# Half-height transposes in two banks and spread inverse sums in an attention and MLP kernel

## The chip, the core and the metric

The kernel runs on one core of one Trainium2 chip. Its engines have queues of their own: TensorE (PE, matmuls; PEld are its weight loads), VectorE (DVE), ScalarE (ACT), GpSimd (POOL) and SyncE (SP), which here issues the DMAs. The metric is the device time of one execution in microseconds, lower is better.

## What is computed

Rotary attention over 4 batches, 8 heads, 576 positions and 64 dimensions, then a layer norm and an MLP of 512 to 2,048 to 512 on the joined heads, with a residual:

```python
q_rot, k_rot = (rotate(q), rotate(k))
scores = scale * np.matmul(q_rot, k_rot.transpose(0, 1, 3, 2))
scores = scores - np.max(scores, axis=-1, keepdims=True)
attn = np.exp(scores)
attn = attn / (np.sum(attn, axis=-1, keepdims=True) + 1e-09)
attn_out = np.matmul(attn, v)
x = attn_out.transpose(0, 2, 1, 3).reshape(B, S, H * D)
mu = np.mean(x, axis=-1, keepdims=True)
var = np.mean((x - mu) ** 2, axis=-1, keepdims=True)
xn = (x - mu) / np.sqrt(var + 1e-06) * g_ln
out = x + np.maximum(xn @ w_ch1, 0.0) @ w_ch2
```

## The kernel before

**Attention** (`attention(i)`) runs over 16 pairs of heads, two heads j on partitions 0 to 63 and 64 to 127. A pair has four query tiles c of 128 queries and a last one (c = 4) of 64 queries, in which the two heads share a tile. For each tile TensorE makes the scores (L419, L415 for c = 4) into one `sc` buffer per head, VectorE takes the row maximum (L460), and ACT the exponential with the row sums (L472). The exponentials `p` have queries on partitions, and the product with v needs keys there, so TensorE transposes them: per tile and head four blocks of 128 x 128 into one `t` bank (`tr`, L516), copied out to `pt` by ACT or VectorE (L285 through `cp_`); the 64 keys left over per two tiles (`tail`, L536); and for c = 4 blocks of 64 rows (`last`, L555 and L556). The product with v (`pv`, L604 for the leftover keys, L608 for the others) goes over part a = 0 (256 queries) and a = 1 (320). It is scaled by the inverse sums into `xt` (L618).

**The inverse sums** stand one per partition and are needed along the free axis, the same on 64 partitions. Before: epsilon is added (L482 on ACT, L484 on VectorE), VectorE inverts (L488), TensorE transposes the 4 or 5 columns to rows (L574), they are copied to `row`, written to DRAM (L586), and read back spread over 64 partitions (L596, L598) into `inv`.

**Banks.** The accumulator memory has eight banks. Three score buffers have two each, `t` has two, used in turn by transposes, products with v and row transposes. When the sum for the layer norm of block 0 is made, the third score buffer is given up for two banks `m` (`share`), for layer norm and MLP.

**The MLP.** Tokens stand in five blocks. Block 0 is multiplied plainly in 32 units (`mlp_unit`, L872, 12 matmuls a unit) in between attention; the other four blocks go in pairs after it (L1025). In the background the weights are decoded and split by VectorE, ACT and GpSimd (L748 to L833).

**The order.** The program is a list of tasks with engines, costs in us, due times (`prio`), things waited for (`after`) and banks or buffers that they `take` and `give`. `Plan.run` goes through them in order of due time and starts the first that could start now, and writes its instructions; each engine then keeps that order. `ORDER` is a list of seeds by which due times are shifted.

## Time and profile before

| | us |
|---|---|
| median of 3 runs | 695.56 |
| the runs | 2233.5, 695.04, 695.56 |
| the profiled execution | 695.15 |
| its span, first to last instruction | 693.4 |

| engine | busy us of the span | instructions |
|---|---|---|
| PE | 672.1 (97%) | 3,954 |
| VectorE | 517.1 (75%) | 856 |
| GpSimd | 416.7 (60%) | 318 |
| ACT | 376.3 (54%) | 805 |

Busy is the union of the instructions' durations. TensorE's are pipelined, so a duration holds latency that overlaps the next instruction; the distance between two starts tells what one step costs. A float32 matmul of the program is two instructions in the trace (two passes), a transpose is one. The span has three parts: attention alone up to some 130 us, attention with block 0's MLP units up to 406, and the paired products after that.

### The profile page before, as it was taken

To read this page: it belongs to the slowest core of one execution; us is meant where nothing else is said; L and a number is where in the kernel's file an instruction comes from. 1 tells how busy PE (TensorE), PEld (TensorE's weight loads), DVE (VectorE), ACT (ScalarE), POOL (GpSimd) and SP (SyncE) were. 2 spreads that over 40 slices of the span, in tenths; PEclk is the share of its full clock that TensorE was granted. 3 is DMA by queue.
4 is the path that set the end of the run, shared out by engine and by line. 5 is a ranking of instruction groups with operands and counts; after the bars stand their busy time and mean duration, and the time that the engine had idled before them with its cause. 6 is when DMAs were issued, how large, how long until landed. Compare 5 with 4: busy or idle time off the path is not lost.

```text
span 693.4 us, 11541 instructions
## 1 busy us (share of the span) xinstructions
PE 672.1 (97%) x3954; PEld 507.2 (73%) x3954; DVE 517.1 (75%) x856; ACT 376.3 (54%) x805; POOL 416.7 (60%) x318
## 2 busy tenths in 40 slices
PE   6989999999999999999999999999999999999997
PEld 5555555666666666666666669989999999999996
DVE  4788878787877777778776758886867868757574
ACT  2677768766669675778675644341434234414130
POOL 4568775667779498787793614761457717415153
PEclk8899999999999999999999999999999999999999
DMA  8355664545847776577675347659668886666663
GB/s 267 123 186 175 200 218 164 176 158 185 293 159 249 252 239 243 174 248 251 242 238 196 108 152 244 214 184 307 215 215 264 268 268 208 221 215 212 213 213 133
DMA packets 85323, 147.20 MB, mean 212 GB/s; under 512 B 10880, under 2 KB 56592, under 8 KB 85264
## 3 DMA queue, kind: packets, MB, share of 16 engines
q1 hardware_dynamic: 85264, 146.45, 63.7%
q8 instruction: 32, 0.52, 0.3%
q14 instruction: 27, 0.22, 0.1%
HBM read 108.60 MB, written 37.82 MB: 211 GB/s over the span
## 4 chain that ended last, share of the span: by engine, by line
PE 88%; DVE 5%; ACT 4%; issue 1%; DMA 1%; SPq 1%; DVEq 0%; ACTq 0%
PE n L1025 40%; PE m L872 12%; PE sc L419 9%; PE t L608 8%; PE t L516 8%; PE sc L415 3%; PE t L604 2%; DVE mx L460 1%; ACT p L472 1%; PE t L555 1%; PE t L536 1%; ACT pt L285 1%; PE m L668 1%; DVE total L484 1%; DVE ws L833 1%
## 5 line engine op out<-in xcount | busy, mean ns | idle before, releaser
L1025 PE MATMUL n<-x,w 128*128 128x448 f32 x672 | 140.2, 367 | 0.0
L1025 PEld LDWEIGHTS n<-x,w 128*128 128x128 f32 x672 | 125.5, 188 | 12.2 <-issue 1.1
L460 DVE TENSOR_REDUCE mx<-sc 128x1 f32<-128x576 f32 x144 | 104.6, 750 | 32.1 <-PE sc L419 24.9
L472 ACT ACTIVATE p<-sc,mx 128x576 f32<-128x576 f32 x144 | 106.0, 740 | 32.1 <-DVE mx L460 27.5
L1025 PE MATMUL n<-o,w 128*128 128x448 f32 x576 | 121.3, 369 | 0.0
L1025 PEld LDWEIGHTS n<-o,w 128*128 128x128 f32 x576 | 107.8, 188 | 11.2 <-issue 0.5
L952 ACT ACTIVATE o<-tmp 128x448 fp32r<-128x448 f32 x96 | 55.3, 579 | 105.4 <-PE n L1025 38.8
L959 POOL TENSOR_TENSOR o<-tmp,o 128x448 fp32r<-128x448 f32 x53 | 66.3, 1269 | 43.8 <-ACT o L952 43.7
L419 PE MATMUL sc<-xk,xq 64*128 64x288 f32 x512 | 85.8, 438 | 4.3 <-DVE xk L338 3.0
L516 PE MATMUL t<-ident,p 128*128 128x128 f32 x512 | 78.3, 285 | 7.0 <-DVE pt L285 1.9
L516 PEld LDWEIGHTS t<-ident,p 128*128 128x128 f32 x512 | 57.0, 143 | 37.9 <-issue 12.6
L285 ACT COPY pt<-t 128x512 f32<-128x512 f32 (+1 forms) x99 | 54.4, 552 | 53.9 <-PE t L516 46.8
L757 POOL TENSOR_TENSOR fw<-fw,w 128x512 int32<-128x512 int32 x32 | 42.9, 1345 | 46.4 <-ACT w L751 20.9
L608 PE MATMUL t<-pt,v 128*64 128x320 f32 (+1 forms) x512 | 69.1, 412 | 0.0
L419 PEld LDWEIGHTS sc<-xk,xq 64*128 64x128 f32 x512 | 48.2, 190 | 25.8 <-issue 10.6
L1097 DVE TENSOR_TENSOR xt<-xt,n 128x448 f32<-128x448 f32 x80 | 48.5, 615 | 18.7 <-PE n L1025 18.4
L608 PEld LDWEIGHTS t<-pt,v 128*64 128x64 f32 x512 | 33.9, 136 | 31.3 <-issue 12.3
L872 PE MATMUL m<-xh,w 128*128 128x512 f32 x128 | 47.8, 417 | 0.0
L872 PE MATMUL m<-hh,w 128*128 128x512 f32 x128 | 47.7, 416 | 0.0
L1084 POOL TENSOR_TENSOR tmp<-tmp 128x448 f32<-128x448 f32 x15 | 20.3, 1354 | 44.9 <-DVE tmp L1063 39.8
L388 POOL TENSOR_TENSOR xs<-xs,rope_sb 128x576 f32<-128x576 f32 x30 | 45.0, 1505 | 1.4 <-DVE mx L460 1.4
L285 DVE COPY pt<-t 128x512 f32<-128x512 f32 (+1 forms) x61 | 37.0, 613 | 10.2 <-PE t L516 6.6
(119 smaller groups left out, 1149.7 us busy)
## 6 DMA issues: line engine op xcount, KB each, us to landing
w<-s SPq DMA_DIRECT2D x64, 512.0 KB
w<-v SPq DMA_DIRECT2D x96, 256.0 KB
s<-ws SPq DMA_DIRECT2D x32, 512.0 KB
xs<-in_qk SPq DMA_DIRECT2D x30, 288.0 KB
w<-in_w1p SPq DMA_DIRECT2D x16, 512.0 KB
v<-w SPq DMA_DIRECT2D x16, 512.0 KB
w<-in_w2p SPq DMA_DIRECT2D x16, 512.0 KB
v<-in_vp SPq DMA_DIRECT2D x16, 320.0 KB
```

Source lines behind the costliest of these rows:

```text
L285: (ACT.copy if plan.engine == "ACT" else DVE.tensor_copy)(o, i)
L388: eng().tensor_tensor(out=x[step], in0=x[step], in1=rope_sb[:, step], op=ALU.mult)
L419: PE.matmul(ps[:, a, :HS], lhsT=q[r, c * P : (c + 1) * P], rhs=k[r, KEYS[a]], start=True, stop=True)
L460: DVE.tensor_reduce(out=mx, in_=st["ps", i, n][:, :, :HS], axis=AX.XY, op=ALU.max, negate=True)
L472: ACT.activation(out=halves(p), in_=st.pop(("ps", i, n))[:, :, :HS], func=AF.Exp, bias=st.pop(("mx", i, n)), scale=1.0, accum_out=total)
L516: PE.transpose(ps[:, k], p[:, j, j * T + k * P : j * T + (k + 1) * P], ident)
L608: PE.matmul(ps[r], lhsT=v[:, k, r], rhs=pt[:, j, k], start=False, stop=k == 3)
L872: PE.matmul(ps, lhsT=wt, rhs=x, start=c + m == 0, stop=c + m == NC + 1)
L952: ACT.activation(out=o[0], in_=x(), func=AF.Relu if relu else AF.Copy)
L959: eng().tensor_tensor(out=lo, in0=x(), in1=raw(hi), op=ALU.subtract)
L1025: PE.matmul(ps, lhsT=wt, rhs=x, start=fresh and kc + z == 0, stop=kc + z == 3, skip_group_check=True)
L1097: DVE.tensor_tensor(out=o, in0=o, in1=ps(which, h), op=ALU.add)
```

## The change

- A tile's transposes of both heads become one task. Each 128 x 128 block is transposed as two halves of 64 rows (64 queries), the first on the array's upper 64 rows into bank 0 of a fixed tile `turned`, the second on the lower 64 rows into bank 1. The group takes both `t` banks; each half is copied out by an instruction of its own. The tails and the last tile are made in the same manner.
- The inverse sums are spread by products: the column of inverses, repeated 64 times, is the stationary operand and the identity the moving one (`spread`, L612 and L615 of the new program), and one copy brings the result to `inv`. Row transposes, row copies and the DRAM round trip go.
- The leftover keys of the product with v are multiplied per head, 64 output columns at a time, like the other keys.
- From pair 4 on, spread products and products with v take `m` banks instead of `t`. `m` is made when the scores of pair 3 are done.
- The planner has modes of the array, S (64 rows), V (64 columns) and M (whole), with costs of a change, and prefers to stay in one; costs are set anew, and `ORDER` is another list with other kinds of shifts.

```diff
--- before.py
+++ after.py
+ROWS = slice(0, D), slice(D, 2 * D)
...
 ORDER = [
...
-SHARE = 0.08, 0.01, 0.1, 0.3, 0.3
+SHARE = 0.08, 0.01, 0.1, 0.3, 0.3, 1.0, 1.0
 OVER = {"PE": 0.0, "DVE": 0.08, "ACT": 0.1, "POOL": 0.045, "NONE": 0.0}
+SWITCH = {("S", "M"): 0.2, ("M", "S"): 0.19, ("S", "V"): 0.3, ("V", "S"): 0.2, ("V", "M"): 0.2, ("M", "V"): 0.1}
+RUN = {"M": 5.0, "S": 0.0, "V": 0.0}
+STAY = {"M": 0.0, "S": 8.0, "V": 8.0}
...
+                if e == "PE":
+                    if kept is None and t.mode != mode:
+                        kept = t, e, picked
+                        most = float("inf") if now - since < RUN[mode] else t.prio + STAY[mode]
+                        continue
+                    if kept is not None and (t.mode != mode or t.prio > most):
+                        continue
...
+                if e == "PE":
+                    t.end += SWITCH.get((mode, t.mode), 0.0)
+                    since, mode = now if mode != t.mode else since, t.mode
...
-    scp, tp = passing("sc", space=PSUM), passing("t", RINGS["t"], space=PSUM)
+    scp, tp = passing("sc", space=PSUM), passing("t", space=PSUM)
+    turned = tp.tile([P, 2, 512], F32, name="t")
...
-    rows = {(i, a): dp.tile([4 + a, P], F32, name=f"sums{i}_{a}") for i in range(NP) for a in range(2)}
...
-            return add({"DVE": 0.19}, g, [add({"ACT": 0.22, "DVE": 0.12}, f, [exps[n] for n in units], N)], N)
+            return add({"DVE": 0.19}, g, [add({"ACT": 0.28, "DVE": 0.16}, f, [exps[n] for n in units], N, port=True)], N)
...
+        ring = "t" if i < NPB else "m"
...
-            qs = slice(c * P - PARTS[a].start, (c + 1) * P - PARTS[a].start)
-            trans = []
-            for j in range(2):
-                def tr(j=j, c=c):
-                    ps = st["tp", i, c, j] = bank_t(i, j).rearrange("p (k n) -> p k n", k=4)
-                    p = st["p", i, c]
+            def tr(c=c):
+                p = st["p", i, c]
+                for j in range(2):
                     for k in range(4):
-                        PE.transpose(ps[:, k], p[:, j, j * T + k * P : j * T + (k + 1) * P], ident)
-                def cp_(j=j, c=c, a=a, qs=qs):
-                    copy(alloc(a)[0][:, j, :, qs], st.pop(("tp", i, c, j)))
-                tt = add({"PE": 0.47}, tr, [exps[2 * c + j]], N + 0.1 * j, take=[ring_t(i, j)], lag=0.2, name=f"t{i}.{c}.{j}")
-                trans.append(tt)
-                take = [f"pt{a}"] if c % 2 == 0 and j == 0 else []
+                        for h, r in enumerate(ROWS):
+                            PE.transpose(turned[:, h, (4 * j + k) * D : (4 * j + k + 1) * D], p[r, j, j * T + k * P : j * T + (k + 1) * P], ident[r, r])
+            def cp_(h, c=c, a=a):
+                at = c * P - PARTS[a].start + h * D
+                copy(alloc(a)[0][:, :, :, at : at + D], turned[:, h].rearrange("p (j k n) -> p j k n", j=2, k=4))
+            tt = add({"PE": 0.47}, tr, [exps[2 * c], exps[2 * c + 1]], N, take=["t", "t"], lag=0.2, name=f"t{i}.{c}", mode="S")
+            trans = [tt]
+            for h in range(2):
+                take = [f"pt{a}"] if c % 2 == 0 and h == 0 else []
                 deps = [tt] + ([parts[a][0]] if parts[a] else [])
...
+                parts[a].append(add(how_c, lambda h=h, f=cp_: f(h), deps, N + 0.1 * h, take=take, give=["t"], of=tt, gid=h, name=f"c{i}.{c}.{h}"))
...
             def tail(c=c):
-                ps = st["tp", i, c, 2] = tp.tile([P, 512], F32, name="t")
                 for n in range(2):
-                    p = st.pop(("p", i, c - 1 + n))
-                    PE.transpose(ps[:, n * P : (n + 1) * P], p.rearrange("p j s -> p (j s)")[:, S - T : S + T], ident)
+                    p = st.pop(("p", i, c - 1 + n)).rearrange("p j s -> p (j s)")
+                    for h, r in enumerate(ROWS):
+                        PE.transpose(turned[:, h, n * D : (n + 1) * D], p[r, S - T : S + T], ident[r, r])
             def tail_copy(c=c, a=a):
-                ps = st.pop(("tp", i, c, 2))
-                copy(alloc(a)[1][:, : 2 * P], ps[:, : 2 * P])
+                o = alloc(a)[1][:, : 2 * P].rearrange("p (n h x) -> p h n x", n=2, h=2)
+                copy(o, turned[:, :, : 2 * D].rearrange("p h (n x) -> p h n x", n=2))
             dep = trans + first_trans + [exps[2 * c + 1], first_exp]
...
+            tt = add({"PE": 0.13}, tail, dep, N + 0.3, take=["t", "t"], give=["p", "p"], lag=0.2, name=f"tl{i}.{c}", mode="S")
+            t2 = add({"ACT": 0.40, "DVE": 0.42}, tail_copy, [tt, parts[a][0]], N + 0.3, give=["t", "t"], of=tt)
             parts[a].append(t2)
...
+        def last():
+            p = st.pop(("p", i, 4))
+            for k in range(4):
+                for j, r in enumerate(ROWS):
+                    PE.transpose(turned[:, j, k * T : (k + 1) * T], p[r, j * T + k * P : j * T + (k + 1) * P], ident[r, r])
+            for j, r in enumerate(ROWS):
+                PE.transpose(turned[0:T, j, 4 * T : 5 * T], p[r, (S - T, 0)[j] : (S, T)[j]], ident[r, r])
+        tt = add({"PE": 0.30}, last, [exps[8]], N, take=["t", "t"], give=["p9"], lag=0.2, name=f"tz{i}", mode="S")
+        for j, r in enumerate(ROWS):
             def last_copy(j=j, r=r):
-                ps = st.pop(("tp", i, 4, j))
                 pt, p4 = alloc(1)
-                copy(pt[:, j, :, 2 * P : 2 * P + T], ps[:, : 4 * T].rearrange("p (k q) -> p k q", k=4))
-                copy(p4[r, 2 * P : 2 * P + T], ps[0:T, 4 * T : 5 * T])
-            tt = add({"PE": 0.42}, last, [exps[8]], N + 0.1 * j, take=[ring_t(i, j)], give=["p9"] if j else [], lag=0.2, behind=[tt] if j else [], name=f"tz{i}.{j}")
+                copy(pt[:, j, :, 2 * P : 2 * P + T], turned[:, j, : 4 * T].rearrange("p (k q) -> p k q", k=4))
+                copy(p4[r, 2 * P : 2 * P + T], turned[0:T, j, 4 * T : 5 * T])
             d = 0.58
...
+            parts[1].append(add({"ACT": d, "DVE": d + 0.05}, last_copy, [tt, parts[1][0]], N + 0.1 * j, give=["t"], of=tt, gid=j))
...
...
+            def one_bank():
+                return turned[:, plan.task.got["t"][0]] if ring == "t" else bank()
+            def spread(a=a):
+                t = st.pop(("sums", i, a))
+                iv = st["spread", i, a] = one_bank()[:, : PARTS[a].stop - PARTS[a].start]
+                for c in range(2):
+                    for j, r in enumerate(ROWS):
+                        PE.matmul(iv[r, c * P : (c + 1) * P], lhsT=t[:, 2 * c + j : 2 * c + j + 1].broadcast_to([P, D]), rhs=ident, start=True, stop=True)
+                if a:
+                    for j, r in enumerate(ROWS):
+                        PE.matmul(iv[r, 2 * P :], lhsT=t[:, 4:5].broadcast_to([P, D]), rhs=ident[:, r], start=True, stop=True)
+            def spread_copy(a=a):
                 if a == 0:
                     st["inv", i] = smp.tile([P, S], F32, name="inv", bufs=RINGS["inv"])
...
+                copy(st["inv", i][:, PARTS[a]], st.pop(("spread", i, a)))
             def pv(a=a):
                 (pt, p4), v = st.pop(("pt", i, a)), st["v", i]
-                s = PARTS[a]
-                ps = st["pv", i, a] = tp.tile([P, s.stop - s.start], F32, name="t")
-                PE.matmul(ps, lhsT=v[:, 4], rhs=p4, start=True, stop=False)
-                for k in range(4):
-                    for j in range(2):
-                        r = slice(j * D, (j + 1) * D)
-                        PE.matmul(ps[r], lhsT=v[:, k, r], rhs=pt[:, j, k], start=False, stop=k == 3)
+                ps = st["pv", i, a] = one_bank()[:, : PARTS[a].stop - PARTS[a].start]
+                for k in range(5):
+                    for j, r in enumerate(ROWS):
+                        PE.matmul(ps[r], lhsT=v[:, k, r], rhs=pt[:, j, k] if k < 4 else p4, start=k == 0, stop=k == 4)
             def scale(a=a):
                 s = PARTS[a]
...
                     DVE.tensor_tensor(out=o, in0=ps[:, x], in1=st["inv", i][:, lo - b * S : hi - b * S], op=ALU.mult)
             N = nominal(i, 3 if a == 0 else 8) + 5
...
+            there = [ev["shared"]] if ring == "m" else []
+            rt = add({"PE": 0.46 if a == 0 else 0.58}, spread, [inverse[a]] + there, nominal(i, 3 if a == 0 else 8) + 0.6, take=[ring], lag=0.2, name=f"sp{i}.{a}", mode="V")
+            rd = add({"ACT": 0.36 + 0.05 * a, "DVE": 0.42 + 0.06 * a}, spread_copy, [rt] + ([rd] if a else []), nominal(i, 3 if a == 0 else 8) + 0.6, take=["inv"] if a == 0 else [], give=[ring], of=rt)
+            t = add({"PE": 2.16 if a == 0 else 2.73}, pv, parts[a] + [ev["v", i]] + there, N, take=[ring], give=[f"pt{a}"] + (["v"] if a else []), lag=0.2, name=f"pv{i}.{a}", mode="V")
             fresh = [n for n, lo, hi in pieces(b, a) if cc == 0 and lo == BLOCKS[n][0]]
             lead = [ev["fresh", n] for n, lo, hi in pieces(b, a) if n not in fresh]
...
+            ev["x", i, a] = add({"DVE": 0.5}, scale, [t, rd], N, behind=lead, take=["xt"] * len(fresh), give=[ring] + (["inv"] if a else []), of=t)
...
-            ev["shared"] = add({"NONE": 0.0}, share, [t3], -1e3, take=["sc"], which=RINGS["sc"] - 1)
-        mt = t = add({"PE": 0.92 * f}, mean, [t3, ev["c3"], ev["shared"]], N, take=["m"], lag=0.2, name=f"ln{n}")
+            pass
+        mt = t = add({"PE": 0.86 * f}, mean, [t3, ev["c3"], ev["shared"]], N, take=["m"], lag=0.2, name=f"ln{n}")
...
     for i in range(1, NP):
+        if i == NPB:
+            ev["shared"] = add({"NONE": 0.0}, share, [ev["s", (i - 1, 4)]], -1e3, take=["sc"], which=RINGS["sc"] - 1)
```

The new order at three places. First TensorE (PE) in the middle of attention, with MLP units around. Before, scores (L419) stand between two groups of whole transposes (L516), then the leftover product (L604) and the others with v (L608):

```order
L516 MATMUL t<-ident,p 128x128 x4
L419 MATMUL sc_115<-xk,xq 128x288
L419 MATMUL sc_114<-xk,xq 128x288
L419 MATMUL sc_115<-xk,xq 128x288
L419 MATMUL sc_114<-xk,xq 128x288
L516 MATMUL t<-ident,p 128x128 x4
L604 MATMUL t<-p_2103,v 128x320
L608 MATMUL t<-pt_2102,v 64x320 x8
L516 MATMUL t<-ident,p 128x128 x4
```

In the changed program the same work, scores (L460), half transposes (L550), product with v (L627), reads:

```order
L460 MATMUL sc_115<-xk,xq 128x288
L460 MATMUL sc_116<-xk,xq 128x288
L460 MATMUL sc_115<-xk,xq 128x288
L460 MATMUL sc_116<-xk,xq 128x288
L550 MATMUL t<-ident,p 128x64 x16
L627 MATMUL m<-pt_1625,v 64x320 x8
L627 MATMUL m<-p_1626,v 64x320 x2
```

Two groups of four whole transposes have become one of 16 halves behind the scores, the product with v goes to `m`, and its leftover keys come last.

Second, TensorE where the inverse sums are turned, before (L574 is the row transpose, L872 an MLP group, L536 a tail of transposes):

```order
L574 MATMUL t<-ident,total_2197 4x128
L872 MATMUL m<-xh,w 128x512
L872 MATMUL m<-xl,w 128x512
L872 MATMUL m<-xh,w 128x512 x2
L872 MATMUL m<-xl,w 128x512
L872 MATMUL m<-xh,w 128x512
L536 MATMUL t<-ident,p 128x128 x2
```

and in the changed program (L550 are half transposes, L612 is the spread product, L891 an MLP group):

```order
L550 MATMUL t<-ident,p 128x64 x16
L612 MATMUL m<-ident,total_1751 64x128 x4
L891 MATMUL m<-xh,w 128x512
L891 MATMUL m<-xl,w 128x512
L891 MATMUL m<-xh,w 128x512 x2
L891 MATMUL m<-xl,w 128x512
```

The row transpose of four columns into a `t` bank has become four products with the identity into an `m` bank, behind a group of half transposes and ahead of the MLP groups.

Third, SP's queue in the early pairs, before (L586 writes rows of sums, L596 and L598 read them back, L739 and L781 move weights, L380 loads q and k):

```order
L739 DMA w_449<-in_w1p 128x1024
L781 DMA v_181<-w 128x1024
L586 DMA sums_1_118<-row_464 5x128
L739 DMA w_511<-in_w1p 128x1024
L596 DMA inv<-sums_1_118 64x2x128
L598 DMA inv<-sums_1_118 64x64
L596 DMA inv<-sums_1_118 64x2x128
L598 DMA inv<-sums_1_118 64x64
L586 DMA sums_0_119<-row_553 4x128
L781 DMA v_182<-w 128x1024
L596 DMA inv<-sums_0_119 64x2x128 x2
```

and in the changed program (L758 and L800 move weights, L421 loads q and k, L439 v):

```order
L800 DMA v_150<-w 128x1024
L758 DMA w_491<-in_w1p 128x1024
L439 DMA v<-in_vp 128x640
L758 DMA w_598<-in_w1p 128x1024
L421 DMA xk<-in_qk 128x576
L421 DMA xs<-in_qk 128x576
L421 DMA xq<-in_qk 128x576
L421 DMA xs<-in_qk 128x576
```

The loads stand one behind the other, with no transfer of sums between them.

## Rows read from the trace of the kernel before

**Rows 1.** Busy time by stretch: us, then each engine's busy us, TensorE's clock, DMA.

```profile
20.00:100.00 80.00, 73.28 (x501) 44.56 (x497) 67.77 (x117) 59.29 (x141) 57.55 (x41) 0.98 0.58 190
100.00:405.00 305.00, 301.20 (x1963) 196.71 (x1961) 234.25 (x399) 214.96 (x480) 218.98 (x162) 1.00 0.61 209
405.00:665.00 260.00, 260.00 (x1321) 233.77 (x1318) 188.81 (x292) 93.04 (x168) 119.12 (x95) 1.00 0.71 227
```

**Rows 2.** The page's chain that ended last, share of the span by engine.

```profile
PE 88%; DVE 5%; ACT 4%; issue 1%; DMA 1%; SPq 1%; DVEq 0%; ACTq 0%
```

**Rows 3.** The chain from 20 to 100 us, shares by line, largest first.

```profile
by line: PE sc L419 20.3%; PE t L516 16.0%; PE t L608 13.3%; DVE mx L460 7.9%; PE sc L415 5.6%; issue 5.0%; DVE total L484 4.4%; PE t L604 3.9%; DVE pt L285 3.9%; DVE fw L760 3.1%; PE t L536 2.2%; PE t L555 2.0%; DVE fw L823 2.0%; ACT pt L2
```

**Rows 4.** TensorE's longest waits, 20 to 100, then 100 to 405: us, times, longest.

```profile
PE t L516 <- ACT pt L285: 1.4, 2, 1.2
...
PE t L516 <- DVE pt L285: 1.1, 1, 1.1
```

**Rows 5.** TensorE in order of time: start, us, line, out<-in, shapes, count.

```profile
122.44 1.16 PE L697 MATMUL m<-std,quarter 128*128 128x128 f32 x8 [0.42 <-DVE std L692]
...
123.44 0.60 PE L516 MATMUL t<-ident,p 128*128 128x128 f32 x4
123.88 0.38 PE L536 MATMUL t<-ident,p 128*128 128x128 f32 x2
124.19 1.24 PE L419 MATMUL sc<-xk,xq 64*128 64x288 f32 x8
125.36 1.09 PE L516 MATMUL t<-ident,p 128*128 128x128 f32 x8
...
127.81 1.95 PE L608 MATMUL t<-pt,v 128*64 128x256 f32 x16
129.68 1.19 PE L415 MATMUL sc<-xk,xq 64*64 64x288 f32 x8
```

**Rows 6.** TensorE in windows cutting into a score group and a product with v.

```profile
133.57 0.65 PE L419 MATMUL sc<-xk,xq 64*128 64x288 f32 x4
...
133.81 0.41 PE L419 MATMUL sc<-xk,xq 64*128 64x288 f32 x2
...
128.29 0.60 PE L608 MATMUL t<-pt,v 128*64 128x256 f32 x4
...
128.50 0.60 PE L608 MATMUL t<-pt,v 128*64 128x256 f32 x4
```

**Rows 7.** Half transposes, on one row half, then on both, in order of time.

```profile
113.66 0.46 PE L555 MATMUL t<-ident,p 64*128 64x64 f32 x4
113.96 0.22 PE L556 MATMUL t<-ident,p 64*64 64x64 f32 x1
...
136.50 0.28 PE L555 MATMUL t<-ident,p 64*128 64x64 f32 x3
136.56 0.22 PE L556 MATMUL t<-ident,p 64*64 64x64 f32 x1
136.62 0.22 PE L555 MATMUL t<-ident,p 64*128 64x64 f32 x1
136.68 0.22 PE L556 MATMUL t<-ident,p 64*64 64x64 f32 x1
```

**Rows 8.** Groups by line and shape, 100 to 405: busy us, mean ns, idle before.

```profile
L285 DVE COPY pt<-t 128x512 f32<-128x512 f32 x31 | 20.9, 682 | 4.5 <-PE t L516 4.5
...
L484 DVE TENSOR_SCALAR total<-total 128x4 f32<-128x4 f32 x8 | 7.1, 884 | 2.3 <-ACT p L472 2.1
...
L285 DVE COPY p<-t 128x256 f32<-128x256 f32 x14 | 5.9, 420 | 3.9 <-PE t L536 3.8
...
L285 ACT COPY pt<-t 128x512 f32<-128x512 f32 x61 | 35.6, 586 | 37.0 <-PE t L516 36.7
```

**Rows 9.** The chain in order of time, whole program: start, us, what.

```profile
403.99 2.30 PE t L608 x16
...
466.36 223.12 PE n L1025 x1086
```

More of the change, by code (lines that the diff above doesn't have):

```diff
@@ L97, in reorder @@
+        if what in ("wait", "lean"):
+            size *= 0.1
+        together = 2 * chance(seed, 9) - 1
+        for i in range(lo, hi):
             t = tasks[i]
-            if later and "SP" not in t.how:
+            if what == "release" and "SP" not in t.how:
                 continue
-            k = kind[i] + 1000003 if mode in (0, 4) else i
-            if chance(seed, 2 * k + 100) < SHARE[mode]:
+            if what == "lean" and len(t.how) == 1:
+                continue
+            if what == "wait" and t.how.keys() in ({"SP"}, {"NONE"}):
+                continue
+            if mode == 6 and kind[i] != kind[lo]:
+                continue
+            if mode >= 5:
+                d = size * together
+            else:
+                k = kind[i] + 1000003 if mode in (0, 4) else i
+                if not chance(seed, 2 * k + 100) < SHARE[mode]:
+                    continue
@@ L102, in reorder, with __init__ @@
                 d = size * (2 * chance(seed, 2 * k + 101) - 1)
[L103 to L106 removed]
+            setattr(t, what, getattr(t, what) + d)
+            if what == "wait":
+                t.wait = max(0.0, t.wait)
 class Task:
[L110 removed]
+    def __init__(self, how, fn, after, prio, take, give, lag, release, name, behind, port, over, of, which, gid, mode):
@@ L214, in run @@
+            for r in t.give:
+                back = 0
+                if t.of and r in t.of.got:
+                    ids = t.of.got[r]
+                    back = ids.pop(ids.index(t.gid) if t.gid is not None else 0)
+                slots[r].append((t.end + 0.1, back))
+                slots[r].sort()
+            self.task, self.engine = t, e
+            t.engine = e
+            self.trace(t.fn)
+            waiting.remove(t)
         self.length = max(t.end for t in self.tasks)
@@ L576, in row_copy @@
-            def row_copy(a=a):
-                row = st["row", i, a] = smp.tile([4 + a, P], F32, name=f"row{a}", bufs=1)
-                copy(row, st.pop(("rp", i, a))[: 4 + a, 0])
-            N = nominal(i, 3 if a == 0 else 8) + 0.6
-            tt = add({"PE": 0.12}, row_t, [inverse[a]], N, take=["t"], lag=0.2)
-            row_w[a] = add({"ACT": 0.28, "DVE": 0.28}, row_copy, [tt], N, give=["t"])
-        for a in range(2):
-            def write(a=a):
-                SP.dma_start(rows[i, a], st.pop(("row", i, a)))
-            def read(a=a):
-                row = rows[i, a]
+            def one_bank():
+                return turned[:, plan.task.got["t"][0]] if ring == "t" else bank()
```

127 lines of the change are left out of this document (46 added, 81 removed), and 10 rows, old and new, of the table ORDER.

## The prediction

> **What bounds the kernel now.** I read the busy times by stretch first, then the chain that ended last, then TensorE's own waits. By stretch [rows 1], TensorE is busy in 301.2 of the 305 us from 100 to 405 and in all 260 us from 405 to 665. Over the whole program the chain runs through TensorE for 88% of the span [rows 2]. Its busy time counts the latency of its pipeline too, so I look at what is left: 3.8 us idle from 100 to 405, the longest wait 1.1 us [rows 4]. So in that stretch a microsecond of work taken off TensorE's queue is close to a microsecond of time. From 20 to 100 it is looser. TensorE is idle for 6.7 us, its longest kind of wait being for copies of transposes [rows 4], VectorE is busy 67.8 of 80 us [rows 1], and the chain passes through TensorE for only 63% (the seven PE entries of [rows 3]). After the last product with v, which begins at 404 us and takes 2.3, TensorE runs the paired products, 1,344 matmuls of which 1,086 take 223.12 us, 0.205 each [rows 9]; none of them is touched. The question is therefore when attention ends.
>
> **Price of a TensorE step.** Starts tell more than durations. Four whole transposes begin at 123.44 and the next group at 123.88: 0.11 us each, 0.109 with one digit more [rows 5]. Four half transposes that use the same 64 rows begin at 113.66 and the fifth at 113.96. The first step is longer (about 0.11) because the array has just changed its shape; the rest are 0.062 each [rows 7]. The rows that decide the case are those at 136.50: halves of both row groups were queued together, and six begin within 0.18 us: three of L555 from 136.50 on and one of L556 at 136.56, which are two pairs one step apart, then single ones at 136.62 and 136.68 [rows 7]. Two halves on different rows thus go side by side, a pair every 0.062 us.
>
> A change of shape costs as follows. I call S the 64-row operations (scores, half transposes), V those with 64 output columns (products with v), M the full ones. Four pairs of score steps take 1.17 us from 124.19 to the next group [rows 5], while a steady pair takes 0.24 [rows 6], so entering and leaving S cost 0.21 together. The product with v holds 8 pairs in 1.87 us from 127.81 to the next group [rows 5], and a steady pair takes 0.21 [rows 6]: at most 0.19 together for V. Two tail transposes need 0.31 us before the next scores begin, against 2 x 0.109 [rows 5]: leaving M costs 0.09, and entering it should cost about half as much. A change is the leaving of one shape and the entering of another; I take 0.16 for each, with ends of 0.14 and 0.20.
>
> **The change, part by part** (TensorE, whole program, counts from the order of the two programs):
> - Big transposes: 512 whole ones at 0.109 = 55.8 us become 1,024 halves, 512 pairs at 0.062 = 31.7. Saved 24.1.
> - Tails: 64 at 0.109 = 7.0 become 64 pairs = 4.0. Saved 3.0.
> - The last 64 queries: 32 groups of five at 0.31 = 9.9 become 80 pairs = 5.0. Saved 4.9, less where the old halves already met, as at 136.50.
> - Row transposes of the sums: 32 at 0.109 = 3.5 go.
> - Spreading the inverse sums by products with the identity: 128 products of 128 columns, in pairs, with two passes each. A pass of 128 columns takes 0.112 (eight in 1.00 us from 122.44, of which the first is some 0.1 longer after a wait [rows 5]); 64 x 2 x 0.112 = 14.3. Then 32 of 64 columns, 16 x 2 x 0.062 = 2.0. Added 16.3.
> - Products with v: the full-width product of the last 64 keys becomes a pair of halves of the same two passes: 0, and its cover is not needed since the columns streamed are the same.
> - Changes of shape: the order has 284 before and 199 after; 85 x 0.16 = 13.6 saved (11.9 to 17).
>
> The sum is -24.1 - 3.0 - 4.9 - 3.5 + 16.3 - 13.6 = -32.8 us.
>
> What comes against it:
> - Early pairs. A quarter of the saving, 8.2 us, falls to the four pairs before about 100 us, where only 63% of the chain is TensorE: I count 5.2 of it, so +3.0 (ends 0 and 8.2).
> - Both banks. A transpose group now holds both transposing banks until both copies are done, and a group behind it waits. Behind the waiting group stand scores, so ACT and VectorE wait next. A copy of 512 columns takes 0.59 on ACT and 0.68 on VectorE [rows 8]; with the transpose's own tail a group that follows directly is held about 0.8 us. The order has twelve places where one group follows another with nothing between; elsewhere scores (1.17 us [rows 5]), products with v or MLP groups stand between and cover the copies. 12 x 0.8 = 9.6; the floor is 0, as the old order also put three groups on two banks. I take 6, nearer the upper end since nothing covers these twelve.
> - VectorE. It takes 68 of the 128 big copies instead of 45, +15.7 us at 0.68; adding epsilon moves mostly to ACT (21 to 6 on VectorE, ten of them at 0.88 [rows 8], about -10); 13 row copies go (-3.5) and 14 copies of the spread inverses come (about 0.42 each [rows 8], +6). In all about +8 on VectorE and -7 on ACT. From 100 on VectorE would be busy about 240 of 283 us, 85%, the share it has today from 20 to 100. I charge nothing; that is the second rival.
> - The third pair of score banks is given up after the last scores of pair 3, some 25 us earlier than before, when the layer norm of block 0 had its sum. With two buffers a query tile needs scores, two maxima and two exponentials in turn, about 3.9 us, some 18.6 a pair against the present 20: 0, at most 3.
> - DMA. 128 small transfers leave SP's queue, where they stood ahead of loads of q, k and weights and each write waited for its row copy. TensorE waits for no transfer in [rows 4], so 0. The spread product takes over the wait for VectorE's reciprocal; it stands behind transposes, or near a product with v, which gives that time.
>
> Total -32.8 + 3.0 + 6.0 = -23.8 us, against the profiled execution's 695.15 us (span 693.4 and 1.8 around it; the median of the runs is 695.56): 671 us.
>
> The page "TensorE: Matmul & The Clock Gate" of the Trainium skill, section "LDWEIGHTS (loading the stationary operand)", speaks against this change. It says that loading a stationary operand takes time by its columns and not by its rows (128 columns over 1.2, about 107 ns), so that a load on a quarter of the rows is as long as a full one. A half transpose loads 128 columns, so by that rule a pair would take as long as a whole transpose and the big transposes would save nothing; the sum would be about 0 instead of -32.8. The trace does not bear it out: half transposes with loads of 128 columns follow each other at 0.062 us on the same rows [rows 7].
>
> **The rivals.**
> 1. The halves gain nothing: over 32 instructions a pair begins only every 0.109 us, as whole transposes do. Then transposes, tails and last queries stay at 72.7 instead of 40.7 us, +32.0; with no other charge the sum is about -1, with the charges above +8: 698 us. For it: the trace shows the overlap only in short bursts. Against it: two pairs in a row at 0.062 [rows 7]. Chance 0.10.
> 2. VectorE, or the wait for both banks, takes back half: VectorE at 85% runs in order, and maxima delayed by it delay exponentials and scores. Half of 23.8 gives 683 us. For it: from 20 to 100, at that share, 7.9% of the chain is the maxima [rows 3]. Against it: ACT and GpSimd have room, and the change makes ACT lighter. Chance 0.19.
> 3. Slower: from pair 4 on, products with v and spread inverses use the two m banks, which belong to the MLP groups of block 0 and to the layer norm. A product with v holds a bank for 1.9 to 2.3 us plus the scaling. If each of the 32 MLP units waits 0.75 us for a bank the gain is gone; from 1.2 us it is 2% slower; at 1.25, half of such a hold, 711 us. Against it: TensorE has no wait on m for a bank in [rows 4], and the added use is some 9 bank-us in a pair of about 24, of some 48 that two banks have. It would show near the layer norms, which hold one bank for many us. Chance 0.08.
>
> **How the numbers follow.** The forecast, 671 us, has 0.63; its own range is 662 (nothing of the 32.8 lost) to 682. Rival 1 has 0.10, rival 2 0.19, rival 3 0.08. The range 662 to 692 leaves out rival 3 and most of rival 1, about 0.17. About 2% (13.9 us) is what a measurement of this kernel can tell from no change, so faster means below 681.6: nearly all of the forecast and some 0.4 of rival 2, 0.69. Within 2% lie the rest of rival 2, nearly all of rival 1 and a little of the forecast, 0.22. Slower is rival 3 and a tail of rival 1, 0.09.
>
> **What would show it.** In the changed profile a group of 16 half transposes should take about 0.55 us from its start to the next group; 1.0 is rival 1. The last product with v should end near 382 us instead of 406, and the paired products should run at 0.205 us as now. The granted clock should stay at 2.4 GHz from 100 us on, as before [rows 1]. TensorE's waits from 100 on should stay under some 10 us; if they are on the copies (pt) or on maxima through the scores it is rival 2, if on m it is rival 3. The spread products should take 0.45 to 0.6 us a group. What would prove me wrong at the root is a saving of TensorE's work that is there, pair by pair, while attention does not end earlier.

## The result and the profile after

The changed kernel takes 699.18 us (median; 696.41 to 703.64), the kernel before 695.38 in the same conditions: a ratio of 1.0061, interval 1.0036 to 1.0085. The forecast was 671 us. It is the middle case, within 2%, and by the interval a little slower. The profiled execution took 702.97 us, its span is 701.0. It is one of the longest of the 13, so the account by stretch below has 7.8 us to explain (702.97 against 695.15), twice what the medians differ by.

Busy time by stretch, changed kernel, columns as in [rows 1]:

```profile
20.00:100.00 80.00, 62.06 (x597) 38.28 (x596) 50.05 (x92) 45.87 (x113) 48.41 (x37) 0.85 0.42 143
100.00:405.00 305.00, 294.17 (x2698) 199.28 (x2695) 244.50 (x396) 217.59 (x494) 230.96 (x168) 0.98 0.58 202
405.00:665.00 260.00, 259.09 (x1348) 231.73 (x1347) 188.70 (x294) 96.22 (x176) 124.69 (x99) 1.00 0.71 225
```

From 20 to 100 us every engine is busy less than in [rows 1] (TensorE 62.1 instead of 73.3, VectorE 50.1 instead of 67.8), and the granted clock averages 0.85 of 2.4 GHz instead of 0.98. The page of the changed kernel has it in 40 slices of 17.5 us, in tenths (9 is 90% or more):

```profile
PEclk9998887999999999999999999999999999999999
```

The clock lies at the lower level, 1.2 GHz, in single pieces of these slices, from 57.4 to 64.2 us for instance, after waits of 1.40 us (at 55.3) and 0.66 us (at 56.3). So something holds all engines up. Where it happens is told best by one event that each pair has, the scores of its last query tile. TensorE in order of time, pairs 0, 4 and 15, then the first paired product, kernel before:

```profile
26.27 1.19 PE L415 MATMUL sc<-xk,xq 64*64 64x288 f32 x8
...
103.74 1.19 PE L415 MATMUL sc<-xk,xq 64*64 64x288 f32 x8
...
392.18 1.19 PE L415 MATMUL sc<-xk,xq 64*64 64x288 f32 x8
...
406.73 1.52 PE L1025 MATMUL n<-x,w 128*128 128x448 f32 x5
```

The same four in the changed kernel:

```profile
23.28 1.19 PE L456 MATMUL sc<-xk,xq 64*64 64x288 f32 x8
...
122.87 2.18 PE L456 MATMUL sc<-xk,xq 64*64 64x288 f32 x8
...
404.05 1.19 PE L456 MATMUL sc<-xk,xq 64*64 64x288 f32 x8
...
414.11 1.09 PE L1044 MATMUL n<-x,w 128*128 128x448 f32 x4
```

| us | before | changed |
|---|---|---|
| up to pair 0's last scores | 26.3 | 23.3 |
| from there to pair 4's | 77.5 | 99.6 |
| to pair 15's | 288.4 | 281.2 |
| to the first paired product | 14.6 | 10.1 |

Three parts became shorter, by 14.7 us together. Pairs 1 to 4 became 22.1 us longer, and that is the whole loss: TensorE's idle time there went from 6.5 to 22.5 us, its work from 71.0 to 77.1. The paired products are as they were (1,080 in 221.02 us, 0.205 each, as in [rows 9]).

What does TensorE wait for there, and what do the others wait for? The longest waits from 20 to 140 us, changed kernel (us, times, longest), TensorE's, VectorE's, then ACT's. L572 are the tails' half transposes, L627 the products with v, L637 their scaling, and L327 is the line of all copies, `pt` those of big groups, `inv` those of spread sums:

```profile
PE t L572 <- DVE pt L327: 8.6, 7, 2.5
PE t L627 <- DVE pt L327: 2.9, 4, 1.5
...
DVE pt L327 <- PE t L627: 9.4, 2, 5.6
...
ACT inv L327 <- DVE xt L637: 10.2, 5, 5.6
...
ACT pt L327 <- PE t L627: 4.9, 1, 4.9
```

TensorE waits for copies of transposes, as it did for 1.4 us in [rows 4], and now for 20 us in all from 20 to 140 us. The odd rows are the third and the last: a copy of transposes waits for L627, the product with v, whose numbers it does not read. In order of time, TensorE, VectorE and ACT of the changed kernel near 60 us:

```profile
58.15 1.12 PE L550 MATMUL t<-ident,p 64*128 64x64 f32 x16
60.12 4.37 PE L627 MATMUL t<-pt,v 128*64 128x320 f32 x16 [0.85 <-DVE pt L327]
64.33 0.70 PE L627 MATMUL t<-p,v 128*64 128x320 f32 x4
...
59.38 0.69 DVE L327 COPY pt<-t 128x512 f32<-128x512 f32 x1 [0.42 <-PE t L550]
66.49 0.56 DVE L637 TENSOR_TENSOR xt<-t,inv 128x256 f32<-128x256 f32 x2 [4.76 <-ACT p L507]
...
65.08 0.58 ACT L327 COPY pt<-t 128x512 f32<-128x512 f32 x1 [4.95 <-PE t L627]
```

A group of 16 half transposes fills both banks by about 59.3. VectorE copies one bank at once, ending at 60.07. TensorE puts the product with v into that bank at 60.12; as the clock is low here, its first 16 instructions take 4.37 us. ACT's copy of the other bank, which has been full since 59.3, starts only at 65.08, when the product is over, after 4.95 us of waiting. So the next group, the exponentials behind that copy on ACT, and the scores behind those all come late.

The two banks are one tile, `turned`. My reading, which the first experiment tests, is that waits are kept by tile: a later instruction of the program on one bank waits for an earlier one on the other. The trace has two kinds of such ties. In all 16 pairs a group's second copy waits for its first when they are on different engines: of 50 such groups not one has its two copies side by side. In pairs 0 to 3, where spread products and products with v use `t` too, copies also wait for those, and scalings and spread copies for work in the other bank. The planner frees bank by bank and knows neither tie.

### The profile page after: what moved, and what is told of

Same layout as the page of the kernel before. It is cut to its first block, busy times and chain, and to the rows that moved or that the text cites. A ratio compares the mean times of both kernels' runs of the same rounds, so it can differ in the third digit from the quotient of the medians.

```text
span 701.0 us, 13188 instructions
## 1 busy us (share of the span) xinstructions
PE 661.3 (94%) x4882; PEld 509.1 (73%) x4882; DVE 516.0 (74%) x843; ACT 373.7 (53%) x808; POOL 429.8 (61%) x328
## 4 chain that ended last, share of the span: by engine, by line
PE 62%; DVE 4%; ACT 2%; issue 1%; DVEq 0%
PE n L1044 39%; PE m L891 9%; PE m L627 5%; PE sc L460 3%; PE t L550 2%; PE sc L456 1%; PE m L612 1%; PE m L687 1%; DVE pt L327 1%; PE t L572 1%; ACT pt L327 0%; PE m L716 0%; DVE xc L725 0%; DVE xc L694 0%; DVE fw L779 0%
## 5 line engine op out<-in xcount | busy, mean ns | idle before, releaser
L1044 PEld LDWEIGHTS n<-x,w 128*128 128x128 f32 x672 | 125.6, 188 | 12.7 <-issue 1.5
L978 POOL TENSOR_TENSOR o<-tmp,o 128x448 fp32r<-128x448 f32 x57 | 73.6, 1316 | 32.0 <-ACT o L971 31.8
L460 PE MATMUL sc<-xk,xq 64*128 64x288 f32 x512 | 86.9, 445 | 2.5 <-DVE xk L379 1.6
L327 ACT COPY pt<-t 128x512 f32<-128x512 f32 (+1 forms) x79 | 41.8, 534 | 57.6 <-PE t L550 37.7
L327 DVE COPY pt<-t 128x512 f32<-128x512 f32 (+1 forms) x81 | 51.5, 642 | 24.8 <-PE t L627 9.4
L460 PEld LDWEIGHTS sc<-xk,xq 64*128 64x128 f32 x512 | 49.3, 196 | 19.4 <-ACT p L507 5.1
L550 PEld LDWEIGHTS t<-ident,p 64*128 64x128 f32 x1024 | 42.4, 144 | 28.8 <-issue 6.2
L550 PE MATMUL t<-ident,p 64*128 64x64 f32 x1024 | 48.7, 233 | 9.2 <-ACT p L507 3.6
L627 PE MATMUL m<-pt,v 128*64 128x320 f32 (+1 forms) x384 | 52.7, 414 | 1.6 <-issue 1.2
L1103 POOL TENSOR_TENSOR tmp<-tmp 128x448 f32<-128x448 f32 x14 | 17.3, 1240 | 52.0 <-DVE tmp L1082 52.0
L891 PE MATMUL m<-hh,w 128*128 128x512 f32 x128 | 45.9, 411 | 0.4 <-DVE xc L725 0.4
L891 PE MATMUL m<-xh,w 128*128 128x512 f32 x128 | 46.1, 413 | 0.1
L796 POOL TENSOR_TENSOR w<-fw,w 128x512 fp32r<-128x512 f32 x20 | 25.9, 1300 | 28.4 <-ACT w L792 27.1
```

Of the source, the lines that this page charges most:

```text
L327: (ACT.copy if plan.engine == "ACT" else DVE.tensor_copy)(o, i)
L460: PE.matmul(ps[:, a, :HS], lhsT=q[r, c * P : (c + 1) * P], rhs=k[r, KEYS[a]], start=True, stop=True)
L550: PE.transpose(turned[:, h, (4 * j + k) * D : (4 * j + k + 1) * D], p[r, j, j * T + k * P : j * T + (k + 1) * P], ident[r, r])
L627: PE.matmul(ps[r], lhsT=v[:, k, r], rhs=pt[:, j, k] if k < 4 else p4, start=k == 0, stop=k == 4)
L891: PE.matmul(ps, lhsT=wt, rhs=x, start=c + m == 0, stop=c + m == NC + 1)
L978: eng().tensor_tensor(out=lo, in0=x(), in1=raw(hi), op=ALU.subtract)
```

## The experiments

**Two tiles.** The tile is split, and with it the copy of a tail, which becomes two; tasks, costs and so the order of all work stay.

```diff
-    turned = tp.tile([P, 2, 512], F32, name="t")
+    turned = [tp.tile([P, 512], F32, name=f"t{h}") for h in range(2)]
...
-                copy(o, turned[:, :, : 2 * D].rearrange("p h (n x) -> p h n x", n=2))
+                for h in range(2):
+                    copy(o[:, h], turned[h][:, : 2 * D].rearrange("p (n x) -> p n x", n=2))
```

> The two turning banks are two one-bank tiles, as before the change, in place of one tile of two banks; the tail copy becomes two copies; the order of all work is unchanged. Theory A (the one tile ties its banks together: a copy of one bank waits for the other bank's copy on the other engine, and in pairs 0 to 3 for a product with v in the other bank): the last scores of pair 4 start at 103 to 112 us in place of 122.9, PE's wait for copies between 20 and 140 us falls from over 16 us to under 6, the clock in 20 to 140 us is above 0.95, and the time is 674 to 690 us. Theory B (the products with v and the spread need the two banks anyway in pairs 0 to 3, so that the loss is one of banks and not of waits tied together): 694 to 704 us, pair 4's last scores still past 118 us.

679.54 us, 0.9802 of before (0.9772 to 0.9832): 19.6 us less than the changed kernel by the medians, 18 by the two ratios, as the kernel before took 693.98 beside this run and 695.38 beside the changed one. Theory A holds by the time, by pair 4's last scores (102.1 us) and by the clock (0.96 from 20 to 140). One of its signs fails: TensorE's waits for copies there fall from 20 us to 11, not to under 6. The last scores of pairs 0, 4 and 15 and the first paired product, two_tiles:

```profile
20.11 1.19 PE L456 MATMUL sc<-xk,xq 64*64 64x288 f32 x8
...
102.09 1.19 PE L456 MATMUL sc<-xk,xq 64*64 64x288 f32 x8
...
378.23 1.19 PE L456 MATMUL sc<-xk,xq 64*64 64x288 f32 x8
...
388.29 0.88 PE L1045 MATMUL n<-x,w 128*128 128x448 f32 x3
```

Pairs 1 to 4 take 82.0 us instead of 99.6, pairs 5 to 15 take 276.1 instead of 281.2. The same place in order of time, TensorE, VectorE and ACT (line numbers after L576 are one higher):

```profile
70.42 1.17 PE L550 MATMUL t<-ident,p 64*128 64x64 f32 x16
72.17 2.38 PE L628 MATMUL t<-pt,v 128*64 128x320 f32 x16 [0.58 <-ACT pt L327]
...
72.01 0.68 DVE L327 COPY pt<-t 128x512 f32<-128x512 f32 x1
...
71.54 0.59 ACT L327 COPY pt<-t 128x512 f32<-128x512 f32 x1 [1.44 <-PE t L550]
```

The copies now overlap, as in 26 of the 50 groups whose copies are on two engines, and VectorE's runs beside the product with v. By stretch, two_tiles, the two stretches in which attention runs:

```profile
20.00:100.00 80.00, 68.85 (x729) 47.12 (x726) 63.16 (x118) 53.69 (x135) 62.70 (x46) 0.94 0.53 177
100.00:405.00 305.00, 299.89 (x2724) 207.05 (x2724) 246.06 (x410) 222.15 (x514) 226.96 (x165) 1.00 0.60 206
```

The clock is up too, 0.94 from 20 to 100. Pairs 1 to 4 still take 4.5 us more than before the change: TensorE idles 11.2 us there instead of 6.5, in many short waits.

A second look at the same kernel, a single run:

> As two_tiles, a second look in the same conditions, for its spread from run to run: within 1% of two_tiles by either theory.

683.05 us. Pairs 1 to 4 take 81.8 us again:

```profile
24.49 2.18 PE L456 MATMUL sc<-xk,xq 64*64 64x288 f32 x8
...
106.24 1.19 PE L456 MATMUL sc<-xk,xq 64*64 64x288 f32 x8
```

The difference between the two looks lies ahead of pair 0's last scores, which run at the lower clock here (2.18 us instead of 1.19). So the 3 us that the start seemed to gain are not a gain that I count on.

**The list of shifts.** Both lists emptied (`ORDER = []`), to see how much of any difference is the order's.

> The changed kernel with its list of order shifts emptied: the planner's plain order. Theory C (the loss in pairs 1 to 4 comes from the order that the listed shifts give): over 5 us away from 699, and less than 15 us lost in pairs 1 to 4. Theories A and B (it comes from banks): the same loss of about 20 us between the last scores of pair 1 and of pair 4, total 695 to 715 us.

> The kernel before with its list of order shifts emptied, as a base for the one above. Theory C: 700 to 720 us, so that the lists alone can hide or make a difference of this size. Theories A and B: within 5 us of 695 us, since the lists move only priorities of single pieces of work.

749.84 us (1.0796, 1.0763 to 1.0829) and 729.62 us (1.0515, 1.0486 to 1.0545). The lists are worth 51 and 34 us, far more than the change itself; theories A and B had expected 695 to 715 and about 695 us, and miss both. Theory C is right that an order can hide or make a difference of this size, so only kernels in the same order of work can be compared for causes. It is wrong on the loss in pairs 1 to 4, which stays in the plain order, as the last scores of pairs 0 and 4 tell. Kernel before, plain order:

```profile
27.30 1.19 PE L409 MATMUL sc<-xk,xq 64*64 64x288 f32 x8
...
106.54 1.19 PE L409 MATMUL sc<-xk,xq 64*64 64x288 f32 x8
```

That is 79.2 us, against 99.0 in the changed kernel (below). The third kernel is two_tiles with the empty list:

> two_tiles with its list of order shifts emptied, beside the plain orders of the changed kernel (749.8 us) and of the kernel before (729.6 us). If the one tile's tied banks are the loss in whatever order: 720 to 735 us, 15 to 30 below the changed kernel's plain order. If they cost only in the listed order: 743 to 755 us.

724.20 us (1.0423, 1.0381 to 1.0464), 25.6 below the changed kernel in the same plain order, within the 15 to 30 of tied banks. Last scores of pairs 0 and 4, plain order, changed kernel:

```profile
23.73 1.51 PE L450 MATMUL sc<-xk,xq 64*64 64x288 f32 x8
...
122.77 1.19 PE L450 MATMUL sc<-xk,xq 64*64 64x288 f32 x8
```

and with two tiles:

```profile
23.62 1.32 PE L450 MATMUL sc<-xk,xq 64*64 64x288 f32 x8
...
107.78 1.19 PE L450 MATMUL sc<-xk,xq 64*64 64x288 f32 x8
```

99.0 against 84.2 us: the ties cost 14.9 us here, 17.6 in the listed order. They are the cause of most of the 19.8 and 22.1 us in either.

**Which tie.** The third score buffer is given up at the start, and spread products and products with v take `m` in all pairs, with one tile and with two. Of the work in the other bank, copies can then only wait for copies.

```diff
-        ring = "t" if i < NPB else "m"
+        ring = "m"
...
+    ev["shared"] = add({"NONE": 0.0}, share, [], -1e3, take=["sc"], which=RINGS["sc"] - 1)
```

> The changed kernel (one tile of two banks), but the third score buffer is given up at the start and the spread and the products with v take m banks in all 16 pairs, so that only transposes use the two turning banks: no copy waits for a product with v any more, but a group's second copy still waits for its first. The list of shifts then fits less. Only to be read against m_two, which has the same order of work. If the waits of copy on copy are most of the loss: 12 to 20 us over m_two. If it is the waits of copies for products with v in pairs 0 to 3: 3 to 7 us over m_two (the 5 us that pairs 4 to 15 lost in the changed kernel against two_tiles, 281.2 against 276.1, and a third of that again for pairs 0 to 3).

> m_one with two one-bank tiles, in the same order of work. By both theories faster than m_one, by 12 to 20 us or by 3 to 7 us. Against two_tiles (679.5 us) it says what two score buffers and a list of shifts that doesn't fit cost: 690 to 730 us.

722.68 us (1.0417, 1.0385 to 1.0449) and 709.94 us (1.0236, 1.0203 to 1.0269): 12.7 us apart, at the lower end of what "copy on copy is most of the loss" was to give. In m_one no two copies of a group run side by side (0 of 52 on two engines), in m_two 30 of 52 do. Where the 12.7 us lie says more than the sum. The waits in brackets are for a score buffer, as two are left. Last scores of pairs 0, 4 and 15, m_one:

```profile
28.46 1.19 PE L456 MATMUL sc<-xk,xq 64*64 64x288 f32 x8 [1.70 <-ACT p L507]
...
122.81 1.19 PE L456 MATMUL sc<-xk,xq 64*64 64x288 f32 x8 [0.77 <-ACT p L507]
...
424.30 1.19 PE L456 MATMUL sc<-xk,xq 64*64 64x288 f32 x8 [0.43 <-ACT p L507]
```

and m_two:

```profile
27.05 1.19 PE L456 MATMUL sc<-xk,xq 64*64 64x288 f32 x8 [1.69 <-ACT p L507]
...
117.26 1.19 PE L456 MATMUL sc<-xk,xq 64*64 64x288 f32 x8 [0.78 <-ACT p L507]
...
412.16 1.19 PE L456 MATMUL sc<-xk,xq 64*64 64x288 f32 x8 [0.42 <-ACT p L507]
```

Copy on copy costs 4.1 us in pairs 1 to 4 (94.4 against 90.2) and 6.6 in pairs 5 to 15 (301.5 against 294.9). In the changed kernel the same stretches lost 17.6 and 5.1. So in pairs 5 to 15 copy on copy is the whole, as only that tie is left there; in pairs 1 to 4 some 13 us are left for the ties to the products with v and the spread products. That split is worked out across two orders of work and not measured by itself: the total of m_one and m_two points to copy on copy, the stretches to the other ties, and how the loss of pairs 1 to 4 divides in the changed kernel stays open.

**Halves against whole transposes.** two_tiles, in the same order, with the big groups turned whole.

```diff
-                        for h, r in enumerate(ROWS):
-                            PE.transpose(turned[h][:, (4 * j + k) * D : (4 * j + k + 1) * D], p[r, j, j * T + k * P : j * T + (k + 1) * P], ident[r, r])
+                        PE.transpose(turned[j][:, k * P : (k + 1) * P], p[:, j, j * T + k * P : j * T + (k + 1) * P], ident)
```

> two_tiles with the 64 big groups turned as 8 whole 128x128 transposes into the same two banks, in the same order of all work (each copy then takes one bank's four blocks). Forecast's term for the big transposes (8 x 0.109 against 16 halves in 0.50 us): plus 24 us of TensorE work, some of it in early pairs where PE waits anyway, and two more shape changes for a group: 698 to 716 us. Rival (halves take as long as whole ones): 677 to 683 us.

698.78 us (1.0055, 1.0030 to 1.0079): the halves are worth 19.2 us by the medians, 17.6 by the ratios to the kernel before. The rival that halves take as long as whole ones falls: TensorE's time for the big transposes is 65.4 us here and 42 in two_tiles, changes of shape at their ends included (237 changes up to the first paired product here, 181 there). The page "TensorE: Matmul & The Clock Gate" of the Trainium skill, section "LDWEIGHTS (loading the stationary operand)", by which a load costs by its columns whatever its rows, would have had them save nothing; the trace does not agree (65.4 against 42 us). What is left of the change without them (spreading by products, the planner, the new order) gains nothing in this order, which was listed for the halves: 698.8 against 695.4.

**The spread products.** One pair of wide products in place of several narrow ones; the kernel leaves out the real inverse sums.

```diff
-                for c in range(2):
-                    for j, r in enumerate(ROWS):
-                        PE.matmul(iv[r, c * P : (c + 1) * P], lhsT=t[:, 2 * c + j : 2 * c + j + 1].broadcast_to([P, D]), rhs=ident, start=True, stop=True)
...
+                for r in ROWS:
+                    PE.matmul(iv[r], lhsT=t[:, :1].broadcast_to([P, D]), rhs=quarter.rearrange("p k n -> p (k n)")[:, : iv.shape[1]], start=True, stop=True)
```

> two_tiles with each spread of inverse sums cut to one pair of products of 256 or 320 columns in place of 4 pairs or 4 and 2 (the output is scaled by wrong numbers; same banks, copies and order). If the spread's products are on the path that sets the end, as the forecast's plus 16.3 us for all of them says: about 8 us of them go (16 x 0.20 and 16 x 0.30 us), 671 to 675 us. If they fit into PE's idle time: 678 to 681 us.

679.13 us (0.9770, 0.9735 to 0.9805), as two_tiles. The experiment was badly made: the part has two or three pairs, not four or six, and one wide pair streams as many columns as they do together. TensorE's time for it is the same, 13.9 us instead of 14.1 in pairs 5 to 15. It shows that the price goes by columns and not by instructions; whether the time is on the path stays open.

**A change of shape by itself.**

```diff
+        rows(32)
+        columns(32)
...
+        for _ in range(8):
+            full(1), rows(1)
...
+        for _ in range(8):
+            rows(1), columns(1)
```

> two_tiles with a block of products on constants ahead of all work, to price a shape change by itself: units of 256 columns on the whole array, on 64 rows (a pair side by side) and on 64 columns (a pair), first 32 of a shape in a row, then in turns of 4 and 4 and of 1 and 1. The forecast's price: 0.16 us for a change, so a round of 4 and 4 with its two changes takes 0.32 us more than 4 and 4 of the grouped units. Rival (the price differs by the kinds, or a run shorter than some length pays more): under 0.08 for some kinds and over 0.2 for others, or other prices in turns of one. The whole time is 30 to 80 us longer than two_tiles.

916.97 us in a single run, 237 more than two_tiles instead of 30 to 80: the block took 245 us, since each product is two passes of 0.216. TensorE in order of time: L1175 is the whole array, L1180 the pair on 64 rows, L1185 the pair on 64 columns.

```profile
87.52 14.08 PE L1180 MATMUL t<-quarter,ident 64*128 64x256 f32 x128
101.54 14.03 PE L1185 MATMUL t<-quarter,ident 128*64 128x256 f32 x128
115.50 0.70 PE L1175 MATMUL t<-quarter,ident 128*128 128x256 f32 x2
...
119.15 2.00 PE L1180 MATMUL t<-quarter,ident 64*128 64x256 f32 x16
121.08 0.48 PE L1175 MATMUL t<-quarter,ident 128*128 128x256 f32 x1
...
218.06 0.70 PE L1175 MATMUL t<-quarter,ident 128*128 128x256 f32 x2
218.69 0.70 PE L1180 MATMUL t<-quarter,ident 64*128 64x256 f32 x4
219.32 0.70 PE L1175 MATMUL t<-quarter,ident 128*128 128x256 f32 x2
...
226.92 0.65 PE L1185 MATMUL t<-quarter,ident 128*64 128x256 f32 x4
227.50 0.70 PE L1180 MATMUL t<-quarter,ident 64*128 64x256 f32 x4
```

A unit is two passes of 0.216, 0.43 us; in the long rows it takes 0.44 on the mean (14.02 and 13.96 us for 32, start to start). In turns of one, a unit takes 0.63 on the whole array, 0.63 on 64 rows and 0.58 on 64 columns: a change costs 0.20, 0.20 and 0.15 by the shape that it goes to. Four units on 64 rows take 1.93 from 119.15 to the next, again 0.20 over 4 x 0.43, so the length of the run plays no part. By the starts of the single products, the last pass of a run takes 0.09 us more than the others whatever its shape, and the first 0.10 more on the whole array and on 64 rows, 0.05 on 64 columns: leaving costs what the forecast had for it (0.09), but entering the whole array costs as much, not half. The forecast's 0.16 was a little low, within its ends. The page "TensorEngine Tiling (Array Packing)" of the Trainium skill, section "Key Properties", says that changing the tiling mode drains TensorE; the trace agrees and puts these numbers to it.

**Layout.** two_tiles with `pt` in blocks of 64 queries.

```diff
-                st["pt", i, a] = ptp.tile([P, 2, 4, n], F32, name=f"pt{a}"), ptp.tile([P, n], F32, name=f"p4{a}")
+                st["pt", i, a] = ptp.tile([P, n // D, 2, 4, D], F32, name=f"pt{a}"), ptp.tile([P, n], F32, name=f"p4{a}")
```

> two_tiles with pt laid out in blocks of 64 queries, so that a copy writes one stretch of 512 numbers in place of 8 strips of 64, and the products with v read strips of 64; the same order of work. If strips cost the copies time: copies from 0.53 and 0.64 us to under 0.50 and 0.60, and 674 to 678 us. If not, or if the products with v then read slower: 679 to 685 us.

680.56 us (0.9808, 0.9772 to 0.9845). The copies take 0.586 us on ACT and 0.68 on VectorE in either layout (medians in pairs 5 to 15), so strips cost them nothing. (The expectation's 0.53 and 0.64 were means over copies of two sizes.)

Of the kernels that compute the whole function, two_tiles is the fastest, with this last one beside it. It beats the kernel before by 2.0% (1.7 to 2.3%) and the changed one by 2.6 to 2.8%.

## Why the prediction was wrong

For each TensorE instruction I took the time from its start to the next one's, without the idle time in it, and summed by kind, from the start to the first paired product (us; "other" is scores, products with v, MLP, layer norm and warming up). Each kind holds the changes of shape at its own ends, which the forecast had in one term, so rows compare roughly and the sum exactly:

| | before | two_tiles | difference | forecast |
|---|---|---|---|---|
| big transposes | 64.8 | 41.9 | -22.9 | -24.1 |
| tails | 8.8 | 9.1 | +0.3 | -3.0 |
| last 64 queries | 12.5 | 7.7 | -4.8 | -4.9 |
| rows out, spread in | 4.7 | 20.5 | +15.8 | +12.8 |
| other, with changes of shape | 298.6 | 286.7 | -11.9 | -13.6 |
| work | 389.4 | 365.9 | -23.5 | -32.8 |
| idle | 16.0 | 21.1 | +5.1 | +9.0 |

- **TensorE is the bound, and the halves go side by side: right.** A group takes 0.59 us to the next work (changed kernel, in order of time, forecast 0.55):

```profile
208.84 0.66 PE L550 MATMUL t<-ident,p 64*128 64x64 f32 x16
209.43 0.76 PE L627 MATMUL m<-pt,v 128*64 128x320 f32 x4
```

  The halves gave 17.6 to 19.2 us of the 24.1. Rival 1's number, 698, is near the result by chance: its mechanism is refuted, the time was lost elsewhere.
- **Sum of the work: 9 us too hopeful.** Tails save nothing: four short halves still enter and leave as a group of their own. Spreading with the row transposes that go is 3.0 us dearer than forecast: 20.5 us where 16.3 were allowed, against 4.7 saved where 3.5 were. The term for shapes can't be read off by itself. Its count holds (267 changes before, 181 after, up to the first paired product, with row transposes counted as whole-array), and its price was, if anything, too low. But about half of the removed changes lie in pairs 1 to 4 (60 to 18), and 37 in pairs 5 to 15 (191 to 154), where TensorE is full. The clock has no part in the 9 us: up to the first paired product it was at the lower level for 10 us in either, before pair 0's last scores in the kernel before and in pairs 1 to 4 in two_tiles.
- **"Both banks", +6.0 us: the step that failed.** I counted twelve places where one group follows another, priced each at 0.8 us, which lets the two copies run side by side, and took everything else as covered by the scores or products in between. I did not ask what a copy waits for. The traces have the twelve places: TensorE idles 13.6 us there in the changed kernel and 8.4 in two_tiles, so with untied banks the price was nearly right. Of the 12.9 us by which idle time after 20 us differs between the two, the other 7.7 lie in places I took as covered, 5.6 of them at transposes behind scores. In the changed kernel idle time went from 16.0 to 34.5 us, 18.5 more where 9.0 were allowed (this term and the early pairs together), and 12.5 us more work than in two_tiles came on top (378.4 against 365.9). Of these, 6.4 fall to pairs 1 to 4, which fits the clock: a mean of 0.85 over 80 us is 24 us at the lower level, 0.94 is 10, and 14 us more at half speed are 7 us of work. Over all of attention it was low for 37 us in the changed kernel and 10 in two_tiles; 27 us at half speed are 13.5 us of work, about the 12.5. Together, 31 us, that is more than the 23.5 us of work that two_tiles saves. With the ties gone the allowance was enough: +5.1.
- **"Early pairs", +3.0: a loss where I looked for a smaller gain.** I asked how little of a saving would count there, not what the new sharing of `t` by transposes, spread and products with v could cost.
- **Clock at 2.4 GHz from 100 us on: wrong for the changed kernel** (0.98 on average from 100 to 405), right for two_tiles (1.00).
- **Rival 2** had the right kind, a wait for both banks, but with VectorE's load as its cause and half the gain as its price. VectorE was less busy than before from 20 to 100 us. **Rival 3** did not happen: TensorE's longest wait on `m` from 100 to 405 us is 1.2 us. Nothing points to the score buffer or to DMA, charged at 0: from 20 us to the first paired product no wait of scores for a buffer, and none of TensorE for a transfer, stands among TensorE's waits in the changed kernel. No run tried them in the same order.
- **The check named at the end held:** the work was saved in pairs 5 to 15, and attention still ended late (the last product with v at 414 us instead of 382).

With two tiles the forecast's own sum comes out at -23.5 + 5.1 = -18.4 us, and the profiled executions lie 16.8 apart (678.33 against 695.15).

## What to carry to other kernels

When banks that were separate tiles become one tile, look in the built program at what every reader and writer of one bank now waits for in the other, above all across engines; price that, not only the bank's own hold time. The Trainium skill's page "Perfetto Trace Analysis", section "Matmuls", advises independent groups to rotate through different banks so that evacuation overlaps the next group; here two banks were not enough, they had to be two tiles (679.54 against 699.18 us). A schedule tuned by search is worth more than most edits, so test one part of a change with the order of work held fixed.

## What was not expected of the hardware

- A change of the array's shape costs 0.20 us into the whole array or into 64 rows and 0.15 into 64 columns, whether the run of one shape is one unit or four.
- Through 16 half transposes in a row, the pairs keep their step of 0.062 us: the first and the last start lie 0.44 us apart (changed kernel, group at 208.84).
- In the probe TensorE worked without a gap from 2 to 247 us; its first passes start 0.43 us apart, at half speed, the others of that run 0.216, and the granted clock is 1.00. In the changed kernel, whose first 100 us have gaps, the clock fell to the lower level: 28 us of pairs 1 to 4, against none in the kernel before and 10 in two_tiles. So waits seem to cost twice, once idle and once slow. How much varies: one_pair has the idle time of two_tiles in pairs 1 to 4 (11.2 us) and 3.4 us at the lower level.
